# Clearing the attention stacks with memsets, reordering their loads, and fetching and splitting the last output block in parts

## The chip, the core and the metric

The kernel runs on one core of a Trainium2 chip. The metric is the device time of one execution in microseconds (us); the median of the runs counts. In the profile PE is TensorE's matmuls, PEld its weight loads, DVE is VectorE, ACT is ScalarE, POOL is GpSimd, and SP is SyncE, whose queue issues nearly all DMAs. ACT and POOL have DMA queues of their own.

## What is computed

One input `x` of 2048 rows by 512 columns goes two ways, and a gate mixes the results row by row. Cut to what matters, the reference is:

```python
x = A_x                                              # 1 x 2048 x 512
g = sigmoid((x * gate_w).sum(-1, keepdims=True))
a = einsum("bsd,ed->bse", x, dft_hid_re)             # DFT along the hidden dimension
b = einsum("bsd,ed->bse", x, dft_hid_im)
y = einsum("ts,bse->bte", dft_seq_re, a) - einsum("ts,bse->bte", dft_seq_im, b)
q, k, v = split(x @ wqkv)                            # 32 heads of 16
p = softmax((q @ k.T) * 16 ** -0.5)
o = (p @ v) @ wo
out = g * y + (1 - g) * o
```

All data are float32. The scores are large, so the softmax needs the true row maxima.

## The kernel before

**Number format.** Each matmul factor is held as a high part in fp32r and the rest as a low part, and a product is made of three matmuls: high by high, high by low, low by high. ACT or POOL makes the high part by a cast, DVE or POOL the low part by a subtraction (`hi_lo`, L86; `parts`, L603). For the scores the three products are folded into one matmul of 64 rows: each of 16 head dimensions has four rows in a "stack" (`qs` and `ks`, 128 partitions by 2048, one half of 64 partitions per head of a pair). Rows 0 to 2 of each four hold the high and low parts in the order that `PARTS` says; row 3 holds ones in `ks` and, in `qs`, the negated row maxima, so that a score comes out with its maximum already subtracted. The other fourth rows must be zero. There are two pairs of stacks, `qs0`/`ks0` and `qs1`/`ks1`, used in turn by the 16 head pairs.

**Stages.** First q and k are projected and their parts stored to DRAM (`qk_d`, L136 to L199). Then the stacks are placed in the memory that the first stage leaves, cleared, given their ones, and loaded (L203 to L289): `clear` (L222) copies the constant tile `zero` over every fourth row by a DMA of SP, `load_rows` (L213) issues three DMAs per call, `load_q` (L227) a call of it and, for later pairs, a small clear. Values and the imaginary DFT part follow (L358 to L376), with the first maxima between their products.

**The main stream** (L1040 and on) is one long list of matmuls, cut into sections. A section takes one of the pattern strings of L920 to L924. Each word of a pattern is a slot: `s` is a score matmul with its exponential on ACT (`scores`, L765), `a` is a score tile of the other orientation for the row maxima, reduced by DVE (`a_tile`, L240, reduction at L248). A word of one letter also takes one 64-row product (`d`) of the DFT or of the projection, on the other half of the array; a word of two letters puts two score tiles beside each other. `^` does a deferred step of the maxima; `|` closes the section: it issues what was held back, the sum of the section before (`add_sum` on POOL, L829), the planned steps (`run_plan`, L910), and then the 16 value matmuls of two key blocks (`pv`, L805, matmuls at L815). `valued` counts these key blocks (units), two per section, 512 in all. 12 pairs of sections use `THIN`, 96 `FULL`, 7 `FOURTEEN`, one `TWELVE`, 8 `TEN`; eight sections follow at the end. There are seven PSUM banks for score tiles and value sums, and `bank` (L412) chooses among them by a model of when DVE and ACT will have read them (`dve`, `act`, `read_by`).

**What sets the order.** Each engine works through its own instructions in the order in which the program issues them; SP, too, stops at the first DMA whose wait is not met. `at(u, f)` plans a step for unit `u`, and `run_plan(u)` does all steps up to `u + 1`, by rising unit and, within a unit, in the order of planning. Steps planned so are the loads of the next stacks (L889 to L898, at odd units), the sums and inverses of a block of four head pairs (`sums`, `inverse`), and the three steps of a block of normalised outputs (`block`, L586: load, multiply on POOL, split and store). The store of a finished DFT tile (`yg_d`, L516) is issued at once, behind a POOL addition (L515) for which SP then waits.

**The last output blocks** (`last_block`, L607) have three steps. For the second half of the rows (`hf` = 1, three pairs, as the sixteenth is handled apart) these are at units 486, 489 and 492: clear, twelve loads, each of outputs paired with one of inverse sums; the multiplication on POOL (L616); and two casts and two subtractions on DVE in one go (`parts`). For `hf` = 0 they are at units 500, 503 and 507.

Of the kernel before, what the change touches and what calls it, by code (L numbers as in the profile page):

```python
# [10 lines left out]
F32 = mybir.dt.float32  # L11
F32R = mybir.dt.float32r
# [4 lines left out]
P = 128  # L17
S = 2048
D = 512
H = 32  # L20
DH = 16
NP = H // 2
KT = D // P
NT = S // P
# [8 lines left out]
def mix_kernel(ctx: ExitStack, tc: tile.TileContext, xa_t, xa, wqkv, w_hid, w_seq, wo, gate_w, out):  # L33
# [5 lines left out]
    nc = tc.nc  # L39
# [17 lines left out]
    r_d = [[dram.tile([2, 4, S // 2], F32, name=f"r{hf}{ct}") for ct in range(4)] for hf in range(2)]  # L57
# [145 lines left out]
    qs, ks = [None] * 2, [None] * 2  # L203
# [3 lines left out]
    vt = main.tile([P, NT, NP, 33], F32, name="vt")  # L207
# [5 lines left out]
    def load_rows(p, c, cols, heads=(0, 1)):  # L213


        t = (qs, ks)[c][p % 2]
        h0, n = heads[0], len(heads)
        rows = slice((2 * p + h0) * DH, (2 * p + h0 + n) * DH)
        for i, v in enumerate(PARTS[c]):
            nc.sync.dma_start(t[64 * h0 + i:64 * (h0 + n):4, cols].bitcast(F32), qk_d[c][v, rows, cols])  # L220

    def clear(t, rows, cols):  # L222
        dst = t[rows, cols].bitcast(F32).rearrange("r (n c) -> r n c", c=P)
        src = zero[:dst.shape[0]].bitcast(F32).unsqueeze(1).broadcast_to([dst.shape[0], dst.shape[1], P])
        nc.sync.dma_start(dst, src)
# [53 lines left out]
    ones = st1.tile([4, 2 * D], F32, name="hl", bufs=2)  # L279
    nc.gpsimd.memset(ones, 1.0)  # L280
    for i in range(2):
        for t in (ks[i], qs[i]):
            clear(t, slice(3, P, 4), ALL)
        for tb in range(2):
            nc.gpsimd.dma_start(ks[i][3:P:32, tb * 2 * D:(tb + 1) * 2 * D].bitcast(F32), ones)
        if i == 0:
            load_rows(0, 1, ALL)
            load_q(0, ALL)
    nc.gpsimd.memset(vt[:, :, :, 16:17], 1.0)  # L289
    wos = [staged(wo[:, kt]) for kt in range(KT)]  # L290
    wrs = []
    a_next = 0
# [88 lines left out]
    work = ctx.enter_context(tc.tile_pool(name="work", bufs=1, side="right", reuse_waits="tile"))  # L381
# [28 lines left out]
    now, free, dve, act = 0.0, [0.0] * 7, 0.0, 0.0  # L410
# [94 lines left out]
    def dft_next(c, tt, s, t, chain, yr):  # L505
        if c == 0 and tt == NT - 1:
            nc.sync.dma_start(t.bitcast(F32), b_d[s])
        if s == NT - 1:
            y = work.tile([P, D], F32, name="y", bufs=2)
            if c == 0:  # L510
                nc.scalar.activation(y, chain.ps, AF.Copy, scale=g[:, tt:tt + 1])
                nc.sync.dma_start(yr_d[tt], y)
            else:
                nc.scalar.activation(y, chain.ps, AF.Copy, scale=ng[:, tt:tt + 1])
                nc.gpsimd.tensor_tensor(y, y, yr[0], ALU.add)  # L515
                nc.sync.dma_start(yg_d[tt], y)  # L516
# [12 lines left out]
    def place(i, dt, name):  # L529

        return const.tile([P, 2, 2, 2 * D], dt, name=name, tag=f"xab{i}")

    def tiles(t):
        return [[t[:, v, q * P:(q + 1) * P] for v in range(2)] for q in range(t.shape[2] // P)]

    def end_tiles(i):
        if i == 0:
            t = const.tile([P, 2, KT, D], F32R, name="wo_hl", tag="xab0")
            wos.append(t)
            for kt in range(KT):  # L540
# [28 lines left out]

    def load_o(o, sm, hf, ct, q0, n=4):  # L570

        cols = slice(q0, q0 + o.shape[1])
        for t in (o, sm):
            if n < 4:
                nc.gpsimd.memset(t, 0.0)
        for h in range(2):
            o0 = 48 if h else 0
            for p in [slice(0, 4)] if n == 4 else [slice(i, i + 1) for i in range(n)]:
                r = slice(64 * h, 64 * h + 64) if n == 4 else slice(64 * h + p.start, 64 * h + 64, 4)
                rows = o_d[hf][4 * ct + p.start:4 * ct + p.stop, o0:o0 + 16, cols]  # L580
                nc.sync.dma_start(o[r], rows.rearrange("p d f -> d p f"))
                nc.sync.dma_start(sm[r], r_d[hf][ct][h:h + 1, p, cols].broadcast_to([16, p.stop - p.start, o.shape[1]]))  # L582

    blocks = {}

# [15 lines left out]
    last_o = []  # L601

    def parts(hi, lo, src):  # L603
        nc.vector.tensor_copy(hi, src)
        nc.vector.tensor_tensor(lo, src, hi.bitcast(F32), ALU.subtract)

    def last_block(step, hf, n, eng):  # L607

        if step == 0:
            if not last_o:  # L610
                last_o.append(place(1, F32, "o_raw"))
            t = last_o[0][:, hf]
            load_o(t[:, 0], t[:, 1], hf, 3, 0, n)
        elif step == 1:
            t = last_o[0][:, hf]
            eng.tensor_tensor(t[:, 0], t[:, 0], t[:, 1], ALU.mult)  # L616
        else:
            o = last_o[0][:, hf, 0]
            if hf:
                ts = [work.tile([P, 2, D], F32R, name=f"o_l{x}", tag=x) for x in ("no", "nh")]  # L620
                for i, t in enumerate(ts):
                    parts(t[:, 0], t[:, 1], o[:, i * D:(i + 1) * D])
                oh[hf, 3] = tiles(ts[0]) + tiles(ts[1])
            else:
                t = place(2, F32R, "o_l")[:, 0]
                parts(t[:, 0], t[:, 1], o)
                oh[hf, 3] = tiles(t)
# [247 lines left out]
    def at(u, f, *args):  # L875
        plan.setdefault(u, []).append(partial(f, *args))

    for hf in range(2):
# [10 lines left out]
    for p in range(1, NP):  # L889
        u = 32 * (p - 1)  # L890
        if p > 1:
            at(u - 11, load_q, p, LOW)
            at(u - 5, load_rows, p, 1, LOW)
            at(u - 3, load_rows, p, 1, THIRD)
            if p > 2:
                at(u - 3 if p < NP - 1 else u - 1, load_rows, p, 1, LAST, (1,))
            at(u - 1, load_rows, p, 1, LAST, (0,))
            at(u - 1, load_q, p, HIGH)  # L898
    one = [d_bank]
    last = proj(0, (3,), [o_bank, o_bank, o_bank, o_bank, d_bank, o_bank], range(2, 8))  # L900
    at(456, load_yg, 0, range(4))
    at(481, load_yg, 0, range(4, 8))
    for step, u in enumerate((486, 489, 492)):
        at(u, last_block, step, 1, 3, nc.gpsimd)
    for step, u in enumerate((500, 503, 507)):
        at(u, last_block, step, 0, 4, nc.gpsimd)
    at(499, load_w15)
    lead = a_next
# [10 lines left out]

    FULL = "s a s s a a s s a a s a s a a s |"  # L920
    THIN = "aS s a s a s s a s a s a a sA |"
    FOURTEEN = "s a s a sS ^ a s s a s a aA |", "aS s a a s ^ s a sS s a s a sA |"
    TWELVE = ("sA a s a s ^ s a s a s s a s |",) * 2
    TEN = "aA s s a s ^ s s s a a sS |", "a s a sS a ^ s s s s s aA |"  # L924

# [9 lines left out]
    users, valued = [], 0  # L935
# [68 lines left out]
    def pairs():  # L1004
# [93 lines left out]
```

## Time and profile before

| what | value |
|---|---|
| runs | 1681.66 us median of 3 (1679.83 to 4099.69) |
| profiled execution | 1681.66 us |
| its span, first to last instruction | 1679.4 us |
| mean granted TensorE clock | 0.997 |
| matmuls, share of the span in which PE is busy | 13170, 99% |
| DVE, ACT, POOL busy | 82%, 74%, 45% |
| HBM traffic | 97 GB/s over the span |

How to read it: PE is busy whenever any matmul is in flight, so its share says nothing of how closely the matmuls follow each other. In the main stream the distance from one group of value matmuls (L815) to the next is the length of a section, and it is there that a section's cost shows. An idle time in brackets behind a row is that of the row's engine just before it, with what ended it.

### The profile page before, as it was taken

How to read it: one execution, taken by the hardware profiler on the slowest of the kernel's cores; microseconds unless marked ns; L12 is line 12 of the kernel's file. 1: busy time of each engine (PE TensorE's matmuls, PEld its weight loads, DVE VectorE, ACT ScalarE, POOL GpSimd, SP SyncE). 2: the span in 40 equal slices, each digit the busy share in tenths (PEclk: the TensorE clock that was granted, in tenths of full speed). 3: DMA queues.
4: the chain of work that ended last, by engine and by line, in shares of the span. 5: the costliest groups of instructions: out<-in, count | busy, mean ns of one | idle time of the engine just before them, and what ended most of it. 6: DMA issues, size and time to landing. Idle time of an engine off the chain costs nothing.

```text
span 1679.4 us, 34984 instructions
## 1 busy us (share of the span) xinstructions
PE 1664.1 (99%) x13170; PEld 1001.3 (60%) x13170; DVE 1380.5 (82%) x2298; ACT 1245.9 (74%) x2470; POOL 750.5 (45%) x810
## 2 busy tenths in 40 slices
PE   9999999999999999999999999999999999999998
PEld 7889966655555555555555555555555555555544
DVE  5458788888888888888888888888888888888776
ACT  5212288887777788778777788777877788888985
POOL 1113644544444466445454466544555556322331
PEclk9999999999999999999999999999999999999999
DMA  9953401113211233222236334222132234621114
GB/s 305 335 176 133 163 2 38 29 49 87 61 56 55 87 92 103 69 64 65 71 102 219 87 105 115 69 79 62 56 98 72 79 105 125 238 84 33 34 32 135
DMA packets 90945, 166.70 MB, mean 99 GB/s; under 512 B 21120, under 2 KB 24584, under 8 KB 89624
## 3 DMA queue, kind: packets, MB, share of 16 engines
q1 hardware_dynamic: 86136, 163.68, 31.3%
q8 instruction: 104, 1.70, 0.4%
q0 software_dynamic: 4352, 0.39, 0.2%
q14 instruction: 65, 0.53, 0.1%
q10 hardware_dynamic: 288, 0.39, 0.1%
HBM read 107.73 MB, written 54.52 MB: 97 GB/s over the span
## 4 chain that ended last, share of the span: by engine, by line
PE 96%; DVE 1%; SPq 1%; DMA 1%; POOL 0%; issue 0%; ACT 0%; DVEq 0%; POOLq 0%
PE d L457 38%; PE t L815 27%; PE t L246 11%; PE t L779 9%; PE t L344 5%; PE t L92 2%; PE t L91 2%; PE t L93 2%; PE t L796 1%; PE t L457 1%; DVE mx L248 1%; SPq L220 0%; DMA qs<-qk 0%; DMA raw<-xa_t 0%; SPq L582 0%
## 5 line engine op out<-in xcount | busy, mean ns | idle before, releaser
L248 DVE TENSOR_REDUCE mx<-t 128x1 f32<-128x512 f32 x2016 | 1253.0, 682 | 223.3 <-PE t L246 191.9
L780 ACT ACTIVATE pt<-t 128x512 f32<-128x512 f32 x2048 | 1034.0, 629 | 14.3 <-PE t L246 5.1
L779 PE MATMUL t<-qs,ks 64*128 64x512 f32 x2048 | 734.6, 409 | 3.3 <-DVE mx L248 3.1
L246 PE MATMUL t<-ks,qs 64*128 64x512 f32 x2016 | 684.5, 399 | 2.8 <-DMA qs<-qk 1.9
L457 PE MATMUL d<-xab,ch 64*128 64x512 f32 x2016 | 656.2, 400 | 0.0
L815 PE MATMUL t<-pt,vt 128*32 128x512 f32 x3968 | 478.8, 600 | 0.2
L457 PEld LDWEIGHTS d<-xab,ch 64*128 64x128 f32 x2016 | 358.1, 184 | 143.8 <-issue 97.2
L246 PEld LDWEIGHTS t<-ks,qs 64*128 64x128 f32 x2016 | 364.6, 185 | 83.5 <-ACT pt L780 47.8
L779 PEld LDWEIGHTS t<-qs,ks 64*128 64x128 f32 x2048 | 367.4, 184 | 74.0 <-DVE mx L248 45.0
L457 PE MATMUL d<-xab,cl 64*128 64x512 f32 x1008 | 403.5, 400 | 0.0
L830 POOL TENSOR_TENSOR osum<-osum,oe 128x512 f32<-128x512 f32 x217 | 280.0, 1290 | 137.0 <-ACT oe L824 134.2
L824 ACT COPY oe<-t 128x512 f32<-128x512 f32 x217 | 127.5, 587 | 225.8 <-PE t L815 223.6
L815 PEld LDWEIGHTS t<-pt,vt 128*32 128x32 f32 x3968 | 103.7, 109 | 233.6 <-issue 149.5
L402 POOL CAST ch<-craw 128x512 fp32r<-128x512 f32 x126 | 77.5, 615 | 342.1 <-PE t L779 285.0
L457 PEld LDWEIGHTS d<-xab,cl 64*128 64x128 f32 x1008 | 185.8, 184 | 73.4 <-issue 50.3
L403 POOL TENSOR_TENSOR cl<-craw,ch 128x512 fp32r<-128x512 f32 x126 | 162.4, 1289 | 10.2
L271 POOL DMA_DIRECT2D qs<-mt x132 | 73.8, 565 | 94.2 <-DVE mt L267 79.6
L457 PE MATMUL d<-wo_hl,o_hl 64*128 64x512 f32 x288 | 77.4, 398 | 0.0
L457 PE MATMUL d<-wre,xab 64*128 64x512 f32 x288 | 70.0, 389 | 0.4 <-DVE mx L248 0.4
L457 PEld LDWEIGHTS d<-wo_hl,o_hl 64*128 64x128 f32 x288 | 52.3, 186 | 17.0 <-ACT pt L780 6.7
L457 PEld LDWEIGHTS d<-wre,xab 64*128 64x128 f32 x288 | 53.0, 184 | 4.2 <-DVE mx L248 0.8
L91 PE MATMUL t<-xab,wh 128*128 128x512 f32 x124 | 48.2, 389 | 0.0
(127 smaller groups left out, 943.3 us busy)
## 6 DMA issues: line engine op xcount, KB each, us to landing
craw<-w_seq SPq DMA_DIRECT2D x128, 256.0 KB
qk<-hl SPq DMA_DIRECT2D x32, 512.0 KB
qs<-qk SPq DMA_DIRECT2D x84, 128.0 KB
b<-hl SPq DMA_DIRECT2D x16, 512.0 KB
xab<-b SPq DMA_DIRECT2D x16, 512.0 KB
o<-osum SPq DMA_DIRECT2D x62, 128.0 KB
oh<-nh SPq DMA_DIRECT2D x12, 512.0 KB
o_hl<-oh SPq DMA_DIRECT2D x6, 1024.0 KB
```

Source lines behind the costliest of these rows:

```text
L91: nc.tensor.matmul(ps, sh, mh, start=first, stop=False)
L246: nc.tensor.matmul(ps, qs[p % 2][r, qt * P:(qt + 1) * P], ks[p % 2][r, kb * 512:(kb + 1) * 512], start=True, stop=True)
L248: user = nc.vector.tensor_reduce(mx[p % 2][:, h, qt, kb:kb + 1], ps, AX.X, ALU.max)
L344: i = nc.tensor.matmul(ps[c], st[r], mv[r], start=phase < 2 and j == 0, stop=phase > 1 and j == 11)
L402: nc.gpsimd.tensor_copy(h1, raw)
L403: nc.gpsimd.tensor_tensor(l1, raw, h1.bitcast(F32), ALU.subtract)
L457: i = nc.tensor.matmul(self.ps, st[r], mv[r], start=not self.begun, stop=stop)
L779: nc.tensor.matmul(ps, ks[p % 2][rr, kt * P:(kt + 1) * P], qs[p % 2][rr, q0:q0 + 512], start=True, stop=True)
L780: return nc.scalar.activation(pts[u][:, 2 * qb + h], ps, AF.Exp, bias=0.0, scale=DH ** -0.5)
L815: nc.tensor.matmul(acc[32 * j:32 * j + 32], vt[:, kt, p, h:h + 32], pt[:, j], start=u == us[0], stop=u == us[-1])
L824: nc.scalar.copy(oe, acc)
L830: nc.gpsimd.tensor_tensor(o, o, oe, ALU.add)
```

## The change

**Clears.** The two DMA clears of each pair of stacks are gone. `ks0` is set to zero by a DVE memset, `qs0`, `ks1` and `qs1` by POOL memsets, whole tiles of 128 by 2048 instead of every fourth row. The DMAs that write the ones, on POOL's queue, and the memset of a column of `vt` keep their engine and move behind the memsets.

SP's queue at the hand-over from the first stage, before (`qk1` is the DRAM copy of k, `hl` its parts, `zero` the constant tile, `raw` the staging of weights):

```order
L144 DMA qk1_87<-hl_927 128x2x512
L225 DMA ks0_937<-zero_156 32x16x128
L225 DMA qs0_936<-zero_156 32x16x128
L220 DMA ks0_937<-qk1_87 32x2048 x3
L220 DMA qs0_936<-qk0_86 32x2048 x3
L225 DMA ks1_939<-zero_156 32x16x128
L225 DMA qs1_938<-zero_156 32x16x128
L107 DMA raw_958<-wo 128x512
```

And now:

```order
L144 DMA qk1_87<-hl_927 128x2x512
L220 DMA ks0_937<-qk1_87 32x2048 x3
L220 DMA qs0_936<-qk0_86 32x2048 x3
L107 DMA raw_958<-wo 128x512
L107 DMA raw_960<-wo 128x512
```

The four clears have left the queue, and the loads of the first stacks stand right behind the last store of the first stage.

**Loads and stores.** The stack loads are planned before all else and at even units, so that in a closing section they come ahead of the sums, inverses and blocks of the same unit instead of behind them. The `yg_d` store is planned one section later than its addition. SP's queue at the end of the ninth head pair (`ks0` gets the keys of the tenth pair, `yg` is a DFT tile, `oh` a finished block, `craw` DFT weights), before:

```order
L392 DMA craw_14628<-w_seq 128x512
L516 DMA yg3_125<-y_14680 128x512
L392 DMA craw_14688<-w_seq 128x512
L599 DMA oh11_146<-nh_14691 256x1x512
L220 DMA ks0_937<-qk1_87 16x512 x3
L220 DMA qs0_936<-qk0_86 32x1024 x3
```

And now:

```order
L392 DMA craw_14628<-w_seq 128x512
L392 DMA craw_14687<-w_seq 128x512
L220 DMA ks0_937<-qk1_87 16x512 x3
L220 DMA qs0_936<-qk0_86 32x1024 x3
L225 DMA qs0_936<-zero_156 4x8x128
L602 DMA oh11_146<-nh_14697 256x1x512
```

The last keys no longer stand behind a store of a DFT tile and a store of a block, both of which wait for POOL.

**Patterns.** `FOURTEEN` had two different halves: 12 slots with 7 `s` and 7 `a`, and 13 slots with 9 `s` and 7 `a`. Each had one single slot more than the nine products that it gets. Now both are the same 12 slots with 8 `s` and 7 `a` and nine single slots.

**The last block.** For `hf` = 1 there are six steps, at units 470 (clear), 482 (load outputs), 486 (load inverse sums), 489 (multiply), 491 and 493 (one half each of the split). For `hf` = 0 the two loads are separate but at the same unit. The bank model is told that each half of the split takes DVE nine slots. DVE's order there, before (`mx` are the maxima, `yp_qs0` an output row, `o_lno` and `o_lnh` the halves of the split):

```order
L640 SCALAR_TENSOR_TENSOR yp_qs0_22671<-d_22914,omg_168,yp_qs0_22671 128x512
L248 TENSOR_REDUCE mx1_170<-t_23035 128x1
L248 TENSOR_REDUCE mx1_170<-t_23038 128x1
L248 TENSOR_REDUCE mx1_170<-t_23051 128x1
L248 TENSOR_REDUCE mx1_170<-t_23072 128x1
L248 TENSOR_REDUCE mx1_170<-t_23076 128x1
L604 CAST o_lno_23087<-o_raw_22873 128x512
L605 TENSOR_TENSOR o_lno_23087<-o_raw_22873,o_lno_23087 128x512
L604 CAST o_lnh_23088<-o_raw_22873 128x512
L605 TENSOR_TENSOR o_lnh_23088<-o_raw_22873,o_lnh_23088 128x512
```

And now (`o_l0` and `o_l1` are the halves):

```order
L649 SCALAR_TENSOR_TENSOR yp_qs0_22674<-d_22914,omg_168,yp_qs0_22674 128x512
L607 CAST o_l0_23024<-o_raw_22342 128x512
L608 TENSOR_TENSOR o_l0_23024<-o_raw_22342,o_l0_23024 128x512
L248 TENSOR_REDUCE mx1_170<-t_23038 128x1
L248 TENSOR_REDUCE mx1_170<-t_23041 128x1
L248 TENSOR_REDUCE mx1_170<-t_23054 128x1
L248 TENSOR_REDUCE mx1_170<-t_23075 128x1
L248 TENSOR_REDUCE mx1_170<-t_23079 128x1
L607 CAST o_l1_23090<-o_raw_22342 128x512
L608 TENSOR_TENSOR o_l1_23090<-o_raw_22342,o_l1_23090 128x512
```

The first half has moved ahead of the five maxima of a section, so that only two operations stand between one section's maxima and the next.

The core of the diff:

```diff
     for i in range(2):
-        for t in (ks[i], qs[i]):
-            clear(t, slice(3, P, 4), ALL)
-        for tb in range(2):
-            nc.gpsimd.dma_start(ks[i][3:P:32, tb * 2 * D:(tb + 1) * 2 * D].bitcast(F32), ones)
+        (nc.gpsimd if i else nc.vector).memset(ks[i].bitcast(F32), 0.0)
+        nc.gpsimd.memset(qs[i].bitcast(F32), 0.0)
         if i == 0:
             load_rows(0, 1, ALL)
             load_q(0, ALL)
-    nc.gpsimd.memset(vt[:, :, :, 16:17], 1.0)
+            nc.gpsimd.memset(vt[:, :, :, 16:17], 1.0)
+        for tb in range(2):
+            nc.gpsimd.dma_start(ks[i][3:P:32, tb * 2 * D:(tb + 1) * 2 * D].bitcast(F32), ones)
...
-                nc.sync.dma_start(yg_d[tt], y)
+                if tt < NT - 1:
+                    at(valued + 2, nc.sync.dma_start, yg_d[tt], y)
+                else:
+                    nc.sync.dma_start(yg_d[tt], y)
...
         if step == 0:
-            if not last_o:
-                last_o.append(place(1, F32, "o_raw"))
-            t = last_o[0][:, hf]
-            load_o(t[:, 0], t[:, 1], hf, 3, 0, n)
-        elif step == 1:
-            t = last_o[0][:, hf]
+            last_o.append(place(1, F32, "o_raw"))
+            for v in range(2):
+                nc.gpsimd.memset(last_o[0][:, 1, v], 0.0)
+            return
+        t = last_o[0][:, hf]
+        if step == 1:
+            load_o(t[:, 0], None, hf, 3, 0, n)
+        elif step == 2:
+            load_o(None, t[:, 1], hf, 3, 0, n)
+        elif step == 3:
             eng.tensor_tensor(t[:, 0], t[:, 0], t[:, 1], ALU.mult)
...
-                ts = [work.tile([P, 2, D], F32R, name=f"o_l{x}", tag=x) for x in ("no", "nh")]
-                for i, t in enumerate(ts):
-                    parts(t[:, 0], t[:, 1], o[:, i * D:(i + 1) * D])
-                oh[hf, 3] = tiles(ts[0]) + tiles(ts[1])
+                i = step - 4
+                t = work.tile([P, 2, D], F32R, name=f"o_l{i}", tag=("no", "nh")[i])
+                parts(t[:, 0], t[:, 1], o[:, i * D:(i + 1) * D])
+                dve = max(now, dve) + 9
+                oh.setdefault((hf, 3), []).extend(tiles(t))
...
+    for p in range(2, NP):
+        u = 32 * (p - 1)
+        at(u - 12, load_q, p, LOW)
+        at(u - 6, load_rows, p, 1, LOW)
...
-            at(u - 11, load_q, p, LOW)
-            at(u - 5, load_rows, p, 1, LOW)
...
-    for step, u in enumerate((486, 489, 492)):
+    for step, u in enumerate((470, 482, 486, 489, 491, 493)):
         at(u, last_block, step, 1, 3, nc.gpsimd)
...
-    FOURTEEN = "s a s a sS ^ a s s a s a aA |", "aS s a a s ^ s a sS s a s a sA |"
+    FOURTEEN = ("aS s aS s a s ^ a s a s a sA |",) * 2
```

More of the change, by code (lines that the diff above doesn't have):

```diff
@@ L570, in load_o @@
     def load_o(o, sm, hf, ct, q0, n=4):
[L572 to L575, printed above, removed]
+        cols = slice(q0, q0 + 1024 if o is None else q0 + o.shape[1])
         for h in range(2):
@@ L579, in load_o @@
                 r = slice(64 * h, 64 * h + 64) if n == 4 else slice(64 * h + p.start, 64 * h + 64, 4)
-                rows = o_d[hf][4 * ct + p.start:4 * ct + p.stop, o0:o0 + 16, cols]
-                nc.sync.dma_start(o[r], rows.rearrange("p d f -> d p f"))
-                nc.sync.dma_start(sm[r], r_d[hf][ct][h:h + 1, p, cols].broadcast_to([16, p.stop - p.start, o.shape[1]]))
+                if o is not None:
+                    rows = o_d[hf][4 * ct + p.start:4 * ct + p.stop, o0:o0 + 16, cols]
+                    nc.sync.dma_start(o[r], rows.rearrange("p d f -> d p f"))
+                if sm is not None:
+                    rows = r_d[hf][ct][h:h + 1, p, cols].broadcast_to([16, p.stop - p.start, cols.stop - q0])
+                    nc.sync.dma_start(sm[r], rows)
     blocks = {}
@@ L607, in last_block @@
     def last_block(step, hf, n, eng):
+        nonlocal dve
         if step == 0:
-            if not last_o:
-                last_o.append(place(1, F32, "o_raw"))
-            t = last_o[0][:, hf]
-            load_o(t[:, 0], t[:, 1], hf, 3, 0, n)
-        elif step == 1:
-            t = last_o[0][:, hf]
+            last_o.append(place(1, F32, "o_raw"))
[8 more added lines that the diff above has]
+        elif step == 3:
             eng.tensor_tensor(t[:, 0], t[:, 0], t[:, 1], ALU.mult)
         else:
-            o = last_o[0][:, hf, 0]
+            o = t[:, 0]
             if hf:
-                ts = [work.tile([P, 2, D], F32R, name=f"o_l{x}", tag=x) for x in ("no", "nh")]
-                for i, t in enumerate(ts):
-                    parts(t[:, 0], t[:, 1], o[:, i * D:(i + 1) * D])
-                oh[hf, 3] = tiles(ts[0]) + tiles(ts[1])
+                i = step - 4
[3 more added lines that the diff above has]
+                oh.setdefault((hf, 3), []).extend(tiles(t))
             else:
@@ L876, in at @@
         plan.setdefault(u, []).append(partial(f, *args))
+    for p in range(2, NP):
+        u = 32 * (p - 1)
+        at(u - 12, load_q, p, LOW)
+        at(u - 6, load_rows, p, 1, LOW)
+        if p > 2:
+            at(u - 4 if p < NP - 1 else u - 2, load_rows, p, 1, LAST, (1,))
+        at(u - 4, load_rows, p, 1, THIRD)
+        at(u - 2, load_rows, p, 1, LAST, (0,))
+        at(u - 2, load_q, p, HIGH)
     for hf in range(2):
@@ L887, in mix_kernel @@
                         at(last + du + 8 * half, block, step, hf, ct, half)
-    for p in range(1, NP):
-        u = 32 * (p - 1)
-        if p > 1:
-            at(u - 11, load_q, p, LOW)
-            at(u - 5, load_rows, p, 1, LOW)
[L894 to L898, printed above, removed]
     one = [d_bank]
@@ L902, in mix_kernel @@
     at(481, load_yg, 0, range(4, 8))
-    for step, u in enumerate((486, 489, 492)):
+    for step, u in enumerate((470, 482, 486, 489, 491, 493)):
         at(u, last_block, step, 1, 3, nc.gpsimd)
-    for step, u in enumerate((500, 503, 507)):
+    for step, u in enumerate((500, 500, 503, 507), 1):
         at(u, last_block, step, 0, 4, nc.gpsimd)
```

## The prediction, on record before the result was known

> **What bounds the kernel.** I read the shares of the page first, then the chain of work that ended last, then the waits of PE.
>
> ```profile
> PE 1664.1 (99%) x13170; PEld 1001.3 (60%) x13170; DVE 1380.5 (82%) x2298; ACT 1245.9 (74%) x2470; POOL 750.5 (45%) x810
> PE 96%; DVE 1%; SPq 1%; DMA 1%; POOL 0%; issue 0%; ACT 0%; DVEq 0%; POOLq 0%
> ```
> ```profile
> PE t L779 <- DVE mx L248: 3.1, 1, 3.1
> PE t L246 <- DMA qs<-qk: 1.9, 1, 1.9
> PE t L246 <- DMA ks<-qk: 0.9, 1, 0.9
> PE d L457 <- DVE mx L248: 0.4, 1, 0.4
> ```
>
> PE carries 96% of the chain, so the change gains only where PE waits, where its matmuls follow each other more slowly than they could, or where its clock drops. The first three waits are single events, and each lies at a place that the diff touches. I go through these in order of time, with the patterns as a fourth place.
>
> **Clears of the stacks.** SP's timeline, then PE's, then two steps of the chain of waits, and prices by shape:
>
> ```profile
> 94.94 0.78 SPq L225 DMA_DIRECT2D ks<-zero  x1
> 95.77 0.64 SPq L225 DMA_DIRECT2D qs<-zero  x1
> 96.51 3.91 SPq L220 DMA_DIRECT2D ks<-qk  x3
> 100.47 1.87 SPq L220 DMA_DIRECT2D qs<-qk  x3
> ...
> 107.02 0.49 PE L246 MATMUL t<-ks,qs 64*128 64x512 f32 x2 [1.90 <-DMA qs<-qk]
> ...
> 101.74 5.19 DMA qs<-qk
> ```
> ```profile
> L604 DVE CAST o_l<-o_raw 128x1024 fp32r<-128x1024 f32 x1 | 0.7, 683 | 0.0
> L60 DVE MEMSET zero<- 128x128 f32 x1 | 0.2, 165 | 0.8 <-PEq L1091 0.8
> ...
> L575 POOL MEMSET o_raw<- 128x1024 f32 x2 | 1.9, 960 | 0.0
> ```
>
> PE could have begun its first maxima at 105.12 (107.02 less 1.90) and waited for the last load of `qs0`, issued at 101.74 and landed 5.19 later. The three loads of `ks0` took SP 3.91 where those of `qs0` took 1.87, so something held them, which I take for the clears ahead (their landing, or their small pieces in the queue). The change removes two DMAs of 0.78 and 0.64 ahead of these loads and that landing, and two more clears from the DMA engines behind them. It adds one DVE memset and three POOL memsets of 2048 elements. POOL's price is two times 0.96, or 1.92, each. DVE's lies between two casts of 1024 elements (2 x 0.683 = 1.37) and sixteen memsets of 128 (16 x 0.165 = 2.64); I take 2.0, halfway. [...]
>
> With DVE free at about 95 (its place is behind the last work of the first stage), `ks0` is clear near 97.1, its loads take 1.87 as those of `qs0` did, and the last `qs0` load goes out near 100.2 instead of 101.74: 1.5 earlier. POOL's `qs0` is clear by then also, if the two memsets do not hold each other up; run one after the other they end 1.9 later and the gain is gone. Behind the DVE memset only copies of `vt` wait on that engine, and PE has other banks for those. The other POOL memsets (3.84 for `ks1` and `qs1`) precede work that comes some 15 us later. **Gain 1.5**; ends 0 and 1.9, the whole wait.
>
> **Loads planned first, stores planned later.** At the tenth pair:
>
> ```profile
> 1045.78 0.60 SPq L599 DMA_DIRECT2D oh<-nh  x1
> 1046.47 2.04 SPq L220 DMA_DIRECT2D ks<-qk  x3
> ...
> 1050.76 0.47 PE L246 MATMUL t<-ks,qs 64*128 64x512 f32 x1 [0.91 <-DMA ks<-qk]
> ```
>
> The keys that PE lacks stand behind a block's store, which waits for POOL until 1045.78. The order now has these loads ahead of the store, so they go out at least 0.6 earlier, and as early as PE gives up the old keys. **Gain 0.9**; ends 0.6, the issue of one store, and 1.2, as the matmuls around the gap are drawn apart too. Everywhere else the loads were in time, so being first brings nothing there. What they are put ahead of (sums, inverses, the store of a block) then waits behind loads that themselves wait for PE; the next step of each block is planned at least four units, two sections, later, which is the cover. The later `yg` store costs nothing, since `y` has two buffers.
>
> **The patterns.** From the chain of waits, the value matmuls, which end each section:
>
> ```profile
> 213.66 1.91 PE t L815 x16
> ...
> 274.87 1.85 PE t L815 x16
> ...
> 1457.85 1.86 PE t L815 x16
> ...
> 1484.70 1.91 PE t L815 x16
> ...
> 1490.35 1.85 PE t L815 x16
> 1495.46 1.91 PE t L815 x16
> ...
> 1527.88 1.92 PE t L815 x16
> ...
> 1548.52 1.88 PE t L815 x16
> ...
> 1596.43 1.87 PE t L815 x16
> ```
>
> Thirteen `FOURTEEN` sections take 1527.88 - 1457.85 = 70.03, 5.39 each; of one pair the 16-tile half takes 5.65 and the 14-tile half 5.11. `TEN` (11 slots, 13 tiles) takes (1596.43 - 1548.52) / 10 = 4.79, `THIN` (14 slots, 16 tiles, evenly 8 and 8) (274.87 - 213.66) / 11 = 5.56. So time follows the tiles that DVE and ACT must read more than the slots: 16 tiles cost about the same in 13 and in 14 slots. The new half has 15 tiles, 8 `s` and 7 `a`. Between 5.11 and the even 5.56 that is 5.34. If slots decided, it would be `TEN` and one slot more: a slot there is (4.79 - 1.86 of values) / 11 = 0.27, so 5.06. I take 5.30, near the first since four kinds of section follow it. **Gain 14 x (5.39 - 5.30) = 1.3**; ends +4.6 (all at 5.06) and -3.6 (all at 5.65).
>
> **The last block, first part.** DVE's timeline, POOL's, PE's, then clock by stretches, then the chain:
>
> ```profile
> 1616.41 1.49 DVE L604 CAST o_lno<-o_raw 128x512 fp32r<-128x512 f32 x1
> 1617.93 1.67 DVE L605 TENSOR_TENSOR o_lno<-o_raw,o_lno 128x512 fp32r<-128x512 f32 x1
> 1619.53 1.48 DVE L604 CAST o_lnh<-o_raw 128x512 fp32r<-128x512 f32 x1
> 1621.04 0.69 DVE L605 TENSOR_TENSOR o_lnh<-o_raw,o_lnh 128x512 fp32r<-128x512 f32 x1
> ...
> 1613.97 2.40 POOL L616 TENSOR_TENSOR o_raw<-o_raw 128x1024 f32<-128x1024 f32 x1 [6.08 <-DMA qs<-mt]
> 1616.32 4.41 POOL L830 TENSOR_TENSOR osum<-osum,oe 128x512 f32<-128x512 f32 x3
> ...
> 1622.39 0.79 PE L779 MATMUL t<-qs,ks 64*128 64x512 f32 x1 [3.15 <-DVE mx L248]
> ```
> ```profile
> 1620.00:1625.00 5.00, 2.61 (x13) 1.77 (x17) 3.57 (x6) 1.93 (x5) 0.72 (x1) 0.68 0.00 0
> 1625.00:1630.00 5.00, 5.00 (x28) 1.80 (x25) 2.83 (x5) 1.61 (x4) 0.69 (x1) 0.63 0.02 3
> ```
> ```profile
> 1624.89 3.57 PE t L815 x16
> 1631.04 1.92 PE t L796 x16
> ...
> 1636.63 1.85 PE t L796 x16
> ```
>
> DVE splits the whole block in one go, 5.3 us, beside three POOL sums that had piled up behind a multiplication that came late. No bank is read meanwhile. PE runs on for 2.83 (1616.41 to 1619.24), then idles 3.15, after which the granted clock is down: 0.68 and 0.63 over ten us, and value matmuls of 3.57 in place of 1.9. From 1596.43 to 1631.04 stand six sections, 34.61 where 6 x 4.79 = 28.74 are due. The excess is 5.87: 3.15 of idling, and 2.7 of slow clock.
>
> Now each half stands in a section of its own. It costs between 0.34 + 0.69 = 1.03 (half the wide cast, and the free subtraction) and 1.49 + 1.67 = 3.16 (both at their worst). I take 1.1 to 2.2, since the loads of the outputs start two sections earlier and only six loads are left at the old place, so that the multiplication is done sooner and POOL's sums no longer pile up behind it. That is below the 2.83 that PE bridges, so the idling goes, and the slow clock with it. The memset (1.92 on POOL) moves eight sections forward, where the only POOL work of a section is one sum and a few small steps. **Gain 5.9**; lower end: halves of 3.16 leave 0.3 of idling and, with DVE late into the second half, up to 1.7 there, so 3.9 if the clock holds. Upper end: the section behind 1631.04 takes 5.59, 0.8 above 4.79, which may be the same disturbance; so 6.7. Late next is nothing that the rows show: the `hf` = 0 block keeps its places.
>
> [...]
>
> **Sum.** 1.5 + 0.9 + 1.3 + 5.9 = 9.6. The profiled execution took 1681.66, of which 2.3 lie outside the span of 1679.4; it is itself the median of the runs shown. 1681.66 - 9.6 gives **1672.1**.
>
> **Rivals.** (1) Slots decide the sections: 5.06 each, 3.3 more gain, 1668.8. For it: `TEN` keeps 13 tiles at nearly slot speed; against it: the four kinds of section above. (2) The split halves still hold PE, by the worst costs above: 2.0 of the tail are lost, 1674.1, and if one of these idles drops the clock again, 1676.8. For it: casts beside POOL's sums took 1.49; against it: the sums no longer pile up. (3) The clears are not quicker: the two memsets run one after the other, or the loads wait for the store of k anyway; 1673.6. (4) The other side: in the new sections the value matmuls come to wait for the last of seven maxima. A section would be 1.86 of values, 0.91 until the first tile is ready and 4.28 of maxima (row below), 7.05; 14 of these cost 23.2 more than now, and with the other 8.3 gained the time is 1696.6. It decides from 6.0 a section on (5.39 + 8.3 / 14). Against it stands that same row, a section with seven maxima, in which the values began at 1495.46 while DVE worked until 1497.19.
>
> ```profile
> 1492.91 4.28 DVE L248 TENSOR_REDUCE mx<-t 128x1 f32<-128x512 f32 x7 [0.91 <-PE t L246]
> ```
>
> **Chances.** Forecast 0.57, rival 1 0.15, rival 2 0.13, rival 3 0.10, rival 4 0.05. The first four lie between 1668 and 1677; rival 2 with a clock drop marks the upper end. With the bounds of the terms (gains of 14.4 at most, and of 3 to 5 when two terms fail) and the 1.8 by which two runs shown differ, the range is 1665 to 1679; rival 4 is left out. Two per cent, 33.6 us, is about what a measurement of this kernel can tell from no change. All PE waits together are a fraction of that, and rival 4 stays inside as well: faster 0.01, same 0.97, slower 0.02.
>
> **What would show it.** The wait at the first maxima below 0.5; no wait for `ks` near 1045; sections of `FOURTEEN` all alike at about 5.3; no idling of PE over 1 us in the tail and a clock of 1.00 up to the end. I am wrong if the new sections exceed 5.4, if PE still waits for DVE at the split, or if a stack load stands behind a new wait of SP.

## The result and the profile after

The changed kernel took 1673.38 us, the median of six runs (1672.02 to 1674.87), against 1680.92 for the kernel before (one run of 4099.69 is left out of the ratio): a ratio of 0.9957, 95% interval 0.9944 to 0.9971. By that ratio the gain is 7.2 us, well inside two per cent, and the time is 1.3 above the 1672.1 that was forecast. The profiled execution took 1673.48 with a span of 1671.6; before it was 1681.66 with 1679.4. The spans differ by 7.8, and this is the sum to be explained.

First the chain's shares on the page after, then, of PE's waits, the one that is left at the places of the change:

```profile
PE 98%; DMA 1%; DVE 0%; SPq 0%; ACT 0%; issue 0%; DVEq 0%
```
```profile
PE t L246 <- DMA qs<-qk: 1.0, 1, 1.0
```

PE's share of the chain went from 96% to 98%. The waits for DVE at the split and for the keys of the tenth pair are gone. The wait for `qs` at the first maxima is still there, halved.

The value matmuls mark where the time came from. This is the chain after (L824 is the old L815, L805 the old L796), and two rows of the chain before that the prediction did not show (its values behind the last `FOURTEEN` section, and its last values):

```profile
212.99 1.92 PE t L824 x16
...
1455.95 1.85 PE t L824 x16
...
1525.89 1.85 PE t L824 x16
1531.25 1.85 PE t L824 x16
...
1594.26 1.86 PE t L824 x16
...
1608.64 1.85 PE t L824 x16
...
1622.94 1.92 PE t L805 x16
1628.53 1.85 PE t L805 x16
...
1658.47 1.85 PE t L805 x16
```
```profile
1533.53 1.85 PE t L815 x16
...
1666.60 1.85 PE t L796 x16
```

The lead over the kernel before, read at the same place of both chains, is

| place | before | after | lead |
|---|---|---|---|
| first values | 213.66 | 212.99 | 0.67 |
| first `FOURTEEN` section | 1457.85 | 1455.95 | 1.90 |
| behind the 14 `FOURTEEN` sections | 1533.53 | 1531.25 | 2.28 |
| six sections ahead of the last pair | 1596.43 | 1594.26 | 2.17 |
| first values of the last pair | 1631.04 | 1622.94 | 8.10 |
| last values | 1666.60 | 1658.47 | 8.13 |
| end of the span | 1679.4 | 1671.6 | 7.8 |

So the start gave 0.7, the stream up to the patterns 1.2, the patterns 0.4, the tail 5.9. From the last values to the end the change loses 0.3 (12.8 before, 13.1 after). Both kernels are alike up to the issue of SP's last store, 8.5 behind the last values, so the 0.3 lies behind that issue. The traces of the experiments below narrow it down: the first, with the last block alone, ends as the kernel before does (4.3 behind that issue), and the fourth, with the old planning, as the kernel after (4.6), so neither of these two parts makes it. Which of the others does stays open.

**The start.** SP's queue, DVE, POOL, and a piece of the chain:

```profile
92.03 3.08 SPq L144 DMA_DIRECT2D qk<-hl  x2
97.50 1.80 SPq L220 DMA_DIRECT2D ks<-qk  x3
```
```profile
95.71 1.76 DVE L282 MEMSET ks<- 128x2048 f32 x1 [0.38 <-DMA qk<-hl]
```
```profile
93.21 1.81 POOL L283 MEMSET qs<- 128x2048 f32 x1 [41.31 <-PE t L92]
```
```profile
94.75 2.73 DMA qk<-hl
...
100.62 5.60 DMA qs<-qk
```

The two clears lie on two engines, the one 1.76 and the other 1.81 long, and they do not overlap: POOL's ends at 95.02, DVE's begins at 95.71. The three loads of `ks0` take 1.80 instead of 3.91. The store of k ahead of them could have slowed them before as well, but in experiment 7 three loads that go out beside this store take 1.81; that leaves the DMA clears. But SP now stands still from 95.11 to 97.50, until two things are done at the same moment: the memset of `ks0` (95.71 + 1.76 = 97.47) and the landing of the last store of k (94.75 + 2.73 = 97.48). PE reaches its wait at 105.38 (106.36 less 0.98) and not at 105.12, a difference that is there before the change begins (the last two stores of k go out from 92.03 instead of 91.77). So the wait is 0.9 shorter and the lead at the first values 0.7.

**The tenth pair.** SP's queue after:

```profile
1037.31 1.76 SPq L220 DMA_DIRECT2D ks<-qk  x3
```

The loads of the keys went out at 1037.31 instead of 1046.47, 9 us earlier. The block's store behind them still waits for POOL, until 1044.90, and holds nobody.

**The tail.** DVE, POOL, SP's loads of inverse sums, and one stretch (us, then engines in the order PE, PEld, DVE, ACT, POOL, then PE's clock, DMA share and GB/s):

```profile
1610.42 0.42 DVE L607 CAST o_l<-o_raw 128x512 fp32r<-128x512 f32 x1
1610.87 0.69 DVE L608 TENSOR_TENSOR o_l<-o_raw,o_l 128x512 fp32r<-128x512 f32 x1
```
```profile
1605.04 2.40 POOL L624 TENSOR_TENSOR o_raw<-o_raw 128x1024 f32<-128x1024 f32 x1
```
```profile
1597.29 3.67 SPq L585 DMA_DIRECT2D o_raw<-r  x6
```
```profile
1620.00:1625.00 5.00, 4.90 (x42) 2.29 (x36) 3.14 (x5) 4.84 (x10) 1.29 (x1) 1.00 0.24 53
```

The multiplication is 9 us earlier than before, 2 of them the lead that it already had, and waits for nothing. Each half of the split costs 1.11; the second, from 1614.47, takes as long as the first. The clock stays at 1.00 where it had been 0.68 and 0.63.

Why the multiplication came late before is seen on SP, whose last load of the block was

```profile
1611.33 0.59 SPq L582 DMA_DIRECT2D o_raw<-r  x1
```

The twelve loads stood there one behind the other from 1603.61 to 1611.92, 8.3 us. Now only six are left at this place, and they are out at 1600.96. The clear has moved forward too. Before, it ran from 1602.63 to 1604.48 and was over when the second of the twelve went out, at 1604.51; no run moves it alone.

### The profile page after: what moved, and what is told of

Its sections match the earlier page's. It is cut to its first block, busy times and chain, and to the rows that moved or that the text cites. A ratio compares the mean times of both kernels' runs of the same rounds, so it can differ in the third digit from the quotient of the medians.

```text
span 1671.6 us, 34975 instructions
## 1 busy us (share of the span) xinstructions
PE 1661.8 (99%) x13170; PEld 1000.6 (60%) x13170; DVE 1379.8 (83%) x2299; ACT 1245.5 (75%) x2470; POOL 754.4 (45%) x813
## 4 chain that ended last, share of the span: by engine, by line
PE 98%; DMA 1%; DVE 0%; SPq 0%; ACT 0%; issue 0%; DVEq 0%
PE d L457 36%; PE t L824 28%; PE t L246 12%; PE t L788 10%; PE t L344 5%; PE t L93 2%; PE t L91 2%; PE t L92 2%; PE t L805 1%; PE t L457 1%; DMA qs<-qk 0%; DMA raw<-wqkv 0%; DVE mx L248 0%; PE t L183 0%; DVE yp L649 0%; SPq L220 0%
## 5 line engine op out<-in xcount | busy, mean ns | idle before, releaser
L824 PE MATMUL t<-pt,vt 128*32 128x512 f32 x3968 | 477.1, 598 | 0.0
L824 PEld LDWEIGHTS t<-pt,vt 128*32 128x32 f32 x3968 | 103.6, 109 | 231.6 <-issue 148.9
```

Of the source, the lines that this page charges most:

```text
L824: nc.tensor.matmul(acc[32 * j:32 * j + 32], vt[:, kt, p, h:h + 32], pt[:, j], start=u == us[0], stop=u == us[-1])
```

## The experiments

The theory: four independent gains, of which the tail's is by far the largest, and in the tail the early loads do the work. Rivals were that the division into halves does it, and, for the patterns, that slots count or that ACT or PE sets the section. The experiments ran on several chips, so their times are best compared by the ratios, each against the kernel before on the same chip, and small differences by the sections of the traces.

**1. The last block alone.** The kernel before, with the new `load_o`, `last_block` and its steps:

```diff
-    for step, u in enumerate((486, 489, 492)):
+    for step, u in enumerate((470, 482, 486, 489, 491, 493)):
         at(u, last_block, step, 1, 3, nc.gpsimd)
```

> The kernel before with the new last block alone (six steps, early loads, two halves). If the four parts of the change act apart from each other, the tail's 5.6 us come back whole and nothing else moves: the wait at the first maxima stays at 1.9, the section at the tenth pair at 7.0, the FOURTEEN sections alternate between 5.17 and 5.60, and the time is 1680.9 - 5.6 = 1675.3. Rival: part of the tail's gain came from the other parts (the stores of DFT tiles moved back, the loads moved ahead), then some of the 3.15 of idling or of the slow clock stays and the time is 1677 or more.

It took 1675.1, ratio 0.9964 (0.9951 to 0.9977). The six sections from the chain:

```profile
1595.94 1.86 PE t L821 x16
...
1624.62 1.92 PE t L802 x16
```

They take 28.68, exactly as in the kernel after (1622.94 - 1594.26). The section of the tenth pair stays long, and so do the alternating `FOURTEEN` sections. The tail's gain belongs to the last block alone.

**2. The split in one go, early loads kept.**

```diff
-    for step, u in enumerate((470, 482, 486, 489, 491, 493)):
+    for step, u in enumerate((470, 482, 486, 489, 493)):
...
-                i = step - 4
+                for i in range(2):
```

> The kernel after, but with both halves of the split in one go at unit 493; the early loads stay. Theory A, the early loads made the gain: the multiplication is done early, POOL's sums do not pile up, the casts take 0.42 each, so the whole split takes 2 x (0.42 + 0.69) = 2.2, less than the 2.83 that PE bridged before; PE does not idle over 0.5, the clock stays at 1.00, the time is 1673.4 +- 1. Theory B, the division into halves made it: with the split in one go PE idles 1 to 3 us, the clock falls again, and the time is 1676 to 1679.

It took 1674.08, ratio 0.9957 (0.9942 to 0.9972), the ratio of the kernel after. The first and the last of the four operations of DVE's split, then the chain:

```profile
1614.24 0.42 DVE L607 CAST o_l<-o_raw 128x512 fp32r<-128x512 f32 x1
...
1615.75 0.69 DVE L608 TENSOR_TENSOR o_l<-o_raw,o_l 128x512 fp32r<-128x512 f32 x1
```
```profile
1608.83 1.85 PE t L824 x16
1613.59 1.87 PE t L824 x16
...
1623.65 1.92 PE t L805 x16
```

The whole split takes 2.2 instead of 5.3, PE has no idle time over 0.1 there, and the clock stays at 1.00. The last three sections take 14.82, against 14.30 with the halves (1608.64 to 1622.94 after). So the early loads, with the clear that moved along with them, bring nearly all of the tail's gain, and the division into halves 0.5.

**3. The split in halves, loads and multiplication at their old places.** The bank model's nine slots for each half are in this kernel too.

```diff
-    for step, u in enumerate((486, 489, 492)):
+    for step, u in enumerate((486, 489, 491, 493)):
```

> The kernel before with the split in halves at units 491 and 493, but with the loads and the multiplication at the old units 486 and 489. Theory A (early loads): the first half now stands on DVE ahead of five maxima and waits there for the multiplication that ends near 1616.4, some 4 us after its place near 1611 to 1612; PE idles 2 to 4 us, the clock may fall, and the time is 1680 or more, no better than before. Theory B (halves alone do it): PE idles less than 1, the time is near 1676.

It took 1683.76, ratio 1.0016 (1.0006 to 1.0025): a little longer than before. POOL, DVE, PE's wait and a stretch:

```profile
1619.34 2.66 POOL L833 TENSOR_TENSOR osum<-osum,oe 128x512 f32<-128x512 f32 x2
```
```profile
1619.41 1.47 DVE L604 CAST o_l<-o_raw 128x512 fp32r<-128x512 f32 x1 [3.88 <-POOL o_raw L618]
1620.91 1.63 DVE L605 TENSOR_TENSOR o_l<-o_raw,o_l 128x512 fp32r<-128x512 f32 x1
...
1625.66 0.42 DVE L604 CAST o_l<-o_raw 128x512 fp32r<-128x512 f32 x1
1626.12 0.69 DVE L605 TENSOR_TENSOR o_l<-o_raw,o_l 128x512 fp32r<-128x512 f32 x1
```
```profile
PE t L782 <- DVE mx L248: 5.7, 1, 5.7
```
```profile
1622.00:1627.00 5.00, 3.80 (x19) 1.64 (x23) 4.66 (x8) 1.68 (x3) 0.00 (x0) 0.50 0.00 0
```

The first half now stands on DVE ahead of five maxima and waits 3.88 for a multiplication that is still late; PE idles 5.66 and then runs at half its clock. The six sections of the tail take 36.03 in this profile, against 34.61 before. This settles the rival: halves without early loads lose. It also shows what goes with the slow casts. Beside POOL's two sums the cast takes 1.47 and the subtraction 1.63, and some 5 us later, with POOL idle (0.00 busy from 1622 to 1627), the same two take 0.42 and 0.69. Why they take longer there, no run here shows.

The start of this profile, with the old clears, shows something else (stretch, then wait):

```profile
108.00:112.00 4.00, 3.82 (x20) 3.60 (x22) 1.79 (x3) 0.00 (x0) 1.71 (x3) 0.57 0.87 282
```
```profile
PE t L246 <- DMA qs<-qk: 2.1, 1, 2.1
```

Here PE waited 2.09 at its first maxima, and the clock fell behind this wait as well, to 0.57 over the next four us. The first values come at 216.37, 2.7 later than in the profile of the kernel before. PE came to the wait 0.97 later and waited 0.19 longer; the 1.5 left is an estimate of what the slow clock cost there. This execution took 1685.94, one of the longest of its kernel, so the median may well hold executions without this fall.

**4. The old load planning.** The kernel after, with the stack loads at odd units behind the blocks; the DFT tile's store stays late.

```diff
-        at(u - 6, load_rows, p, 1, LOW)
...
+            at(u - 5, load_rows, p, 1, LOW)
```

> The kernel after with the stack loads planned as before (odd units, behind the blocks); the store of the DFT tile stays one section later. If the place of the loads made the gain at the tenth pair, the section of unit 288 goes back from 5.79 to about 7.0 with a wait of PE for the keys of 0.9, and the time is 1673.4 + 1.3 = 1674.7. Rival: the DFT tile's store, which waited for POOL, was what held the keys; then the section stays near 5.8 and the time at 1673.4.

It took 1674.15. SP's queue, and PE's wait:

```profile
1044.49 0.60 SPq L602 DMA_DIRECT2D oh<-nh  x1
1045.19 2.07 SPq L220 DMA_DIRECT2D ks<-qk  x3
```
```profile
PE t L246 <- DMA ks<-qk: 0.9, 1, 0.9
```

The wait is back, and the section of unit 288 goes from 5.79 to 6.97. The block's store holds the keys; the DFT tile's store is late here too and helps nothing. The whole gain at this place is the loads' place in the queue.

**5. Thirteen slots.**

```diff
-    FOURTEEN = ("aS s aS s a s ^ a s a s a sA |",) * 2
+    FOURTEEN = ("aS s a s s a s ^ a s a s a sA |",) * 2
```

> The kernel after with 13 slots instead of 12 in each FOURTEEN section, at the same 15 tiles (8 s, 7 a; one of the two-letter words taken apart). If the time follows the tiles, the sections stay at 5.35 +- 0.05 and the time at 1673.4. If slots count, each section grows by a slot, 0.27, to 5.62, and the time by 14 x 0.27 = 3.8, to 1677.

It took 1672.71. Twelve sections of its chain, the second to the fourteenth group of values:

```profile
1460.89 1.85 PE t L824 x16
...
1525.61 1.85 PE t L824 x16
```

They take 64.72, against 64.58 after (1461.31 to 1525.89). A slot more costs next to nothing: 0.01 a section, where 0.27 was the rival's.

**6. Which reader sets the section.** Two kernels leave work out of the `FOURTEEN` sections: one half of each maximum's columns, the other most of the copies and additions of the value sums.

```diff
-        user = nc.vector.tensor_reduce(mx[p % 2][:, h, qt, kb:kb + 1], ps, AX.X, ALU.max)
+        user = nc.vector.tensor_reduce(mx[p % 2][:, h, qt, kb:kb + 1], ps[:, :256 if lean else 512], AX.X, ALU.max)
```

> The kernel after with the maxima of the FOURTEEN sections taken over half of each tile's columns (leaves out half of that reduction). DVE is busy 37.2 of 43.1 us there (86%) and would fall to near 55%. If DVE's reading sets the section, it falls from 5.35 to what the slots need, 5.06 to 5.1, and the time by about 14 x 0.27 = 3.8. If ACT's reading or PE itself sets it, the sections stay at 5.3 or more.

```diff
         o = osum[:, hf]
+        if lean and 1 < kt < NT - 1:
+            return
```

> The kernel after without the copy of the value sums by ACT and their addition by POOL in most FOURTEEN sections (leaves out these sums: 10 or 11 of the 14 copies of 0.59). If ACT's reading sets the section, it falls by up to 0.25 to 5.1, and the time by 2.5 to 3. If DVE sets it, or PE, the sections stay at 5.3 or more and the time at 1673.

The first took 1669.73, the second 1672.05. Chain of the first, then of the second, twelve sections each:

```profile
1459.15 1.92 PE t L825 x16
...
1521.05 1.91 PE t L825 x16
```
```profile
1460.15 1.85 PE t L824 x16
...
1524.72 1.85 PE t L824 x16
```

With half the maxima twelve sections take 61.90, against 64.58 after, or 5.16 each; without the copies 64.57, the same as after. So DVE's reading sets these sections, and ACT has slack. In eight of them, after, DVE is busy 37.2 of 43.1 us (86%), not all the time. It is not saturated, but PE needs the banks that it has yet to read: in these eight the weight loads of the score tiles waited 8.7 us for DVE's maxima and 1.2 for ACT's exponentials. Why the section stops at 5.16 and not at the 5.06 to 5.1 expected stays open.

**7. The loads of q ahead of those of k.**

```diff
-            load_rows(0, 1, ALL)
-            load_q(0, ALL)
+            load_q(0, ALL)
+            load_rows(0, 1, ALL)
```

> The kernel after with the first loads of qs0 put ahead of those of ks0. In the kernel after, the loads of ks0 go out at 97.50, when the DVE memset of ks0 (95.71 and 1.76) and the landing of the last store of k are both just done; qs0 was clear at 95.02 and its DRAM copy complete long before. If these two hold SP, the three loads of qs0 now go out from about 95.2 and take the 1.8 that SP stood still, the last load goes out near 98.8 instead of 100.62, and the wait at the first maxima (0.98, 1.02 and 0.20 in three profiles) is gone: 1672.6 or somewhat less. If the bytes in the queue set the landing (six loads of 256 KB), the last load still lands near 106 and the wait stays.

It took 1672.74. SP's queue, the chain and POOL:

```profile
94.75 1.81 SPq L220 DMA_DIRECT2D qs<-qk  x3
```
```profile
94.30 5.50 DMA qk<-hl
```
```profile
99.90 0.58 POOL L287 MEMSET vt<- 128x256 f32 x1 [5.32 <-DMA qk<-hl]
```

The loads went out as expected (q at 94.75, k from 97.05 to 98.77), yet PE still waited 0.69. The last store of k, now beside the loads of q, took 5.50 to land instead of 2.73. The memset of `vt`, which needs the memory that this store reads, waited for it, and the ones of `ks0` stood behind that memset.

**8. The same, with the ones ahead of that memset.**

```diff
+        if i == 0:
+            nc.gpsimd.memset(vt[:, :, :, 16:17], 1.0)
```

> As e7_q_loads_first, with the memset of the vt column on POOL moved behind the ones of ks0. In e7 this memset waited until 99.81 for the landing of the last store of k, and the ones of ks0 stood behind it; the first maxima waited 0.69, which the chain puts down to POOL. Theory: the landing of the ones was the last of the waits. Then the ones go out near 97 instead of 100.50, and PE waits less than 0.2 at its first maxima; time 1672.2, within what two runs differ by. Rival: the loads of ks0, issued from 97.05 to 98.77, land too late; then the wait stays at 0.5 to 0.7.

It took 1672.03 (1671.92 to 1672.6), ratio 0.9939 (0.9924 to 0.9954), span 1670.0. POOL:

```profile
98.02 1.29 POOL L288 DMA_DIRECT2D ks<-hl  x2 [3.07 <-DVE ks L282]
```

The ones went out at 98.02, and no wait over 0.1 is left at the first maxima. One profile alone would not carry this: the wait in the profiles of kernels that load k first was 0.98, 1.01, 0.20, 0.70, 0, 0, 0.77 and 0.93 (mean 0.57). With q first and the ones early it was 0 here and in the last kernel below. As two of the eight were 0 too, two more zeros make it likely, not certain, that the wait is gone. Nor is it shown that the landing of the ones was the last of the waits: in experiment 7 the profile puts PE's wait down to the memset of `qs1` on POOL, which ended at 105.33 there and ends at 104.33 here.

**9. The bank model's nine slots.**

```diff
-                dve = max(now, dve) + 9
```

> The kernel after without the line by which the bank model gives DVE nine slots for each half of the split. If the model's reserve made the section of unit 490 longer (5.20 where 4.78 is due), it goes back to 4.8 and the time falls by 0.4 to 1673.0. If DVE's own 1.1 us of splitting makes it, that section stays at 5.2, or PE waits for a bank there instead and it grows; time the same or up to 0.5 longer.

It took 1672.97. The chain:

```profile
1608.25 1.85 PE t L823 x16
1613.54 1.85 PE t L823 x16
...
1622.65 1.92 PE t L804 x16
```

The section of unit 490 takes 5.29 instead of 5.20, the three sections 14.40 instead of 14.30. The reserve is not what makes it longer than 4.78; it gives 0.1. That leaves DVE's own 1.1 us, and experiment 2 agrees: there this section holds no half of the split and takes 4.76 (1608.83 to 1613.59), and the next, with both halves, 5.68 instead of 4.71.

**10. The maxima bunched at the end.**

```diff
-    FOURTEEN = ("aS s aS s a s ^ a s a s a sA |",) * 2
+    FOURTEEN = ("aS s aS s s a ^ s a s a s aA |",) * 2
```

> The kernel after with the same 12 slots and 15 tiles in each FOURTEEN section in another order: the second two-letter word stays early, two maxima of the first six slots become scores, and the last two words hold three maxima. In e6_half_maxima the sections fell from 5.35 to 5.15 when DVE read half. If DVE's idle time at the head of a section (1.08 or 0.42 before its first tile, while PE does the values) is what it lacks, work left for it there brings the section to 5.15 to 5.25 and the time down by 1.5 to 3. If the order does not matter, or the values then wait for the later tiles, the section stays at 5.35 or grows.

It took 1674.05. Twelve sections:

```profile
1460.98 1.85 PE t L824 x16
...
1526.60 1.85 PE t L824 x16
```

65.62, or 0.09 a section more than after. The expectation was wrong: work left for DVE under the values does not help, and bunched reads cost a little.

**11. The best of these.** Experiment 8, with the last maximum one slot earlier:

```diff
-    FOURTEEN = ("aS s aS s a s ^ a s a s a sA |",) * 2
+    FOURTEEN = ("aS s aS s a s ^ a s a sA a s |",) * 2
```

> e8_q_first_ones_early with one more change: in the FOURTEEN sections the last of the seven maxima stands in the eleventh slot and the twelfth holds a single score, so that the maxima are spread and end earlier (e10, where they ended bunched, took 5.44 in place of 5.35). If the bunching of DVE's reads makes the section, it falls to 5.25 to 5.30 and the time by 0.7 to 1.4 from 1672.0. If not, the sections stay at 5.35 and the time at 1672.0; if ending on a score delays the values behind ACT, they grow to 5.4 or more and the time is 1673.

It took 1671.83 (1671.4 to 1672.25), ratio 0.9951 (0.9937 to 0.9964), span 1669.9. Twelve sections take 64.57 (1459.67 to 1524.24 by the trace), so the order brings nothing. Both this kernel and the eighth beat the kernel before. Against the kernel after their spans are 1.6 and 1.7 shorter, but the intervals of the ratios overlap, and that lead isn't established by the times.

## Why the prediction came out

**Clears: 1.5 forecast, 0.9 in this pair of profiles.** The mechanism was right: DMA clears had slowed the loads behind them (3.91 to 1.80). Whether two memsets would hold each other up was not tried, since POOL's was over before DVE's began. Two sizes were off. The memset began at 95.71, not 95, so the last load went out at 100.62, not 100.2; and that load took 5.60 to land, not 5.19. The memset itself took 1.76, not 2.0. The sum left out that the landing of the last store of k binds at the same moment as this memset, though rival 3 had named this wait; a shorter memset alone would have met it. Of the signs, a wait below 0.5 did not come in this profile. The term varies from one execution to the next: the wait was 1.90, 1.44 and 2.09 in three profiles with the old start, mean 1.81, against the mean of 0.57 above, so 1.2 is the better estimate.

**Loads: 0.9 forecast, 1.2 found**, the upper end. The wait and the drawing apart around it both went, since the loads went out 9 us earlier and not 0.6. The experiment with the old planning shows the cause. Another section, of unit 126, took 5.98 before and 5.81 after; as it is 5.81 with the old planning too, and 6.01 with the last block alone, its 0.17 is not the loads', and stays open.

**Patterns: 1.3 forecast, 0.4 found.** The step that failed is "I take 5.30, near the first since four kinds of section follow it". The interpolation by tiles gave 5.34 and twelve of the sections take 5.35; the shading towards the slots was worth nothing, as a slot more costs 0.01. The other two, the second and the twelfth, take 5.60 and 5.44, which the prediction did not have: fourteen of 5.35 would be 74.9, and they took 75.3 (1455.95 to 1531.25). By the prediction's own sign (over 5.4) these two are misses. With half the maxima both fall to the rest (5.11 and 5.16), so DVE's reading is in it; what more there is in these two stays open. Apart from them the sections did become alike, and rival 4, the values waiting for seven maxima, did not come.

**Last block: 5.9 forecast, 5.9 found** (34.61 to 28.68). The idling and the slow clock went, the halves cost 1.11 each at the lower end of 1.1 to 2.2, and POOL's sums no longer piled up. What the prediction left joined, the runs took apart: the early loads did it, and the halves without them make the kernel slower, with PE held and the clock down as in the worse form of rival 2. The upper end was wrong in its reason: the section behind the first values of the last pair takes 5.59 after as before, so it was no disturbance.

**The clock.** It fell in the kernel before after 3.15 of idling (0.68 and 0.63 over the two stretches of five us from 1620 on), and in the third experiment after 2.09 at the start (0.57 over the next four us) and after 5.66 in the tail (0.50). It did not fall after 1.90 at the start of the kernel before (1.00 over the next four us), nor after 1.44 with the last block alone (0.999 over its whole profile). What decides whether it falls, no run here shows. Of the three waits at the start with the old clears the longest, 2.09, had a fall behind it, and a fall there the prediction did not price.

The size of the gain may thus depend on the clock of the execution that one compares with. The runs without a trace fit this. Of 37 of the kernel before beside the experiments, the two shortest, 1677.57 and 1678.74, have a mean granted clock of 0.999, as the kernel after has, and the six longest, 1682.83 to 1684.45, one of 0.996. The median after lies 4.2 and 5.4 below the two shortest. Without a trace of such an execution this stays a likely reading, not a shown one.

**The sum.** 0.7 + 1.2 + 0.4 - 0.1 + 5.9 - 0.3 = 7.8. The forecast of 9.6 was too large by the patterns (0.9), the clears (0.6 to 0.8) and the end (0.3), less the loads' 0.3; the measured time lies in the range, and two of the terms were wrong in the same direction. A little luck is in the time: the forecast began from an execution of 1681.66, 0.7 above the later median of 1680.92, and that hid as much of the excess.

## What to carry to other kernels

When an operation on a busy engine is long, ask first whether its inputs were late and what piled up beside it; dividing it helps only once they are early, and puts it in front of more work if they are not. Price a section by what its slowest reader must read, and take the interpolated value as it stands. When a wait is removed, look for the one that ends at the same moment, and judge a wait of about a microsecond from several profiles.

## What the runs showed of the hardware

- A cast of 128 x 512 from f32 to fp32r on DVE took 0.42 without additions on POOL and 1.47 to 1.49 beside additions on POOL; the subtraction took 0.69 and 1.63 to 1.67. The multiplication of 128 x 1024 on POOL took 2.40 before and after.
- A memset of 128 x 2048 f32 took 1.76 on DVE and 1.81 to 1.90 on POOL.
- The same store to DRAM took 2.73 to land with no load issued behind it and 5.50 with three loads of 256 KB right behind it.
- The granted clock fell after PE had idled 2.09 (0.57 over the next four us), 3.15 (0.68 and 0.63) and 5.66 (0.50), and not after 1.90 or 0.91 (1.00 over the next four us each).
